# Taking the even part of a sum out of its PSUM bank with ScalarE, and adding the edge product with GpSimd

## The chip, the cores and the metric

The kernel runs on one core of one Trainium2 chip. The metric is the device time of one execution in microseconds (us). Every ratio below is to the kernel before, run on the same chip in the same rounds.

The engines are called by the names in the profile: PE is TensorE (PEld its weight loads), DVE is VectorE, ACT is ScalarE, POOL is GpSimd, SP is the engine whose queue issues transfers.

## The reference

An input of 8 x 3008 x 256 goes through a two-dimensional Fourier transform, of which the real part is kept, and then through a feed-forward layer with a squared relu:

```python
X = np.fft.fft(x, axis=1)
X = np.fft.fft(X, axis=2)
x = X.real.reshape(8 * 3008, 256)
h = np.maximum(x @ w_in, 0.0)         # w_in: 256 x 2048
out = (h * h) @ w_out                 # w_out: 2048 x 256
```

The real part of row k and that of the mirrored row S - k are, but for an edge term, an even part plus or minus an odd part. So the kernel works on half of the rows and makes the hidden values of a row and of its mirror from the same two products.

## The kernel before

The second transform is folded into the weights: `G1` holds the even (cosine) combination of `w_in`, `G2` the odd (sine) one, and `G3` is -2 times `G2` with its edge row set to zero. `PQ[b][0]` and `PQ[b][1]` are the even and odd parts of the transformed input. Row pairs are worked in chunks of 512 (`CH`; two chunks of 256 at the start, a short one of 264 at the end). A chunk has 16 units `u`, one per 128 hidden features. Its 128 or so matmuls of the second product (`po`) are interleaved with those of the first (`xb`) of the next chunk, so that PE never has to stop (it has no idle time from 100 to 600 us).

A unit in `x_front` costs PE three matmuls of 512 columns into one bank: even, odd, then, after ACT has read the bank with a relu, -2 times odd into the same bank, which ACT reads again for the mirror. A unit in `x_split` costs PE only two, into two banks, and pays for it on ACT and DVE:

```python
def x_front(c, u):                                   # cut
    for sn, G in ((0, G1), (1, G2)):
        mm(xb[...], G[:, fs], PQ[b][sn][...], ...)
    act(r_s(c, u), xb, AF.Relu)                      # L605
    return (c, u, xb, None)

def x_split(c, u):                                   # cut
    xs = [psx.tile([P, 512], F32, name=nm, tag="x")[:, 0:n] for nm in ("xo", "xe")]
    for t, G, sn in ((xs[0], G2, 1), (xs[1], G1, 0)):
        mm(t[...], G[:, fs], PQ[b][sn][...], ...)
    act(bs[0], xs[0], AF.Copy, bias=0.0, scale=1.0)  # L629

    def add():                                       # one step later
        stt(out=bs[1], in0=ebc[c][:, 0:n], scalar=gE2[:, u : u + 1], in1=bs[0], op0=ALU.mult,
            op1=ALU.subtract)                        # L632
        def sat(o, t):                               # L636: min(max(in0 + in1, 0), BIG)
            nc.vector._custom_dve(TENSOR_ADD_SAT, out=o, in0=xs[1], in1=t, s0=BIG, s1=0.0)
        sat(r_s(c, u)[:, 0, :], bs[0])
        relu_d(c, u, lambda o, i: sat(o[:, 0, :], bs[1]))

def x_back(cur):                                     # two steps later, cut
    if xb is None: return
    mm(xb[...], G3[:, fs], PQ[b][1][...], False, True)
    relu_d(c, u, lambda o, i: act(o, xb[:, :, i], AF.Relu))     # L651

def x_square(cur):                                   # per two units, cut
    if u // 2 in PLAN[c][1]: ...                     # a few on ACT, in two halves
    else: vt(h2, h2, h2, op=ALU.mult)                # L663, 128 x 2048, SBUF to SBUF

YZ = [(0, 0)] * 3 + [(2, 0)] * 3 + [(5, 1)] * 9 + [(7, 1)] * 9 + [(0, 0)]
```

`YZ` says how many of a chunk's 16 units are split, chunk by chunk: none, 2, 5, 7. `ebc[c]` is the edge row of the odd part, broadcast to all partitions by a transfer on POOL's queue, and `gE2` the edge weights.

## Time and profile before

| | before |
|---|---|
| time | 630.06 us (629.28 to 631.47, 4 runs) |
| PE busy, share of the span | 96% |
| DVE, ACT, POOL busy | 85%, 76%, 11% |
| units split (two matmuls instead of three) | 114 |

These lines are from the page of the kernel before: the busy times, the busy tenths of 40 slices for PE and DVE, the chain of waits, and the groups of instructions (line, engine, operation, out<-in, shapes, count | busy us, mean ns | idle time of the engine ahead of them).

```profile
PE 606.4 (96%) x4682; PEld 446.9 (71%) x4682; DVE 536.8 (85%) x827; ACT 479.3 (76%) x872; POOL 68.8 (11%) x97
...
PE   3969999999999999999999999999999999999997
...
DVE  8788799995988989889899879998999899999920
...
PE 92%; DVE 6%; ACT 1%; issue 0%; DVEq 0%; POOL 0%; POOLq 0%; ACTq 0%
...
L663 DVE TENSOR_TENSOR h<-h 128x2048 f16<-128x2048 f16 (+1 forms) x174 | 207.8, 1195 | 41.1 <-ACT h L651 36.5
...
L636 DVE CUSTOM_DVE_ANT_0 h<-xe,bs 128x512 f16<-128x512 f32 x228 | 145.9, 680 | 0.0
...
L632 DVE SCALAR_TENSOR_TENSOR bs<-eb,gE,bs 128x512 f32<-128x512 f16 x114 | 85.0, 745 | 9.1 <-ACT bs L629 8.4
L629 ACT ACTIVATE bs<-xo 128x512 f32<-128x512 f32 x114 | 68.5, 601 | 21.0 <-PE xo L73 16.3
```

PE is at nine tenths or more in all but three slices (the first, the third and the last), and the chain that ended last is 92% PE: the kernel is bound by TensorE. The mean of a saturating add is 680 ns, of the edge operation 745, of a square 1195 over all shapes (1219 for the full shape in the middle of the run). A split unit therefore costs DVE about 2.1 us and ACT a copy of 0.60 us, and saves PE one 512-column matmul.

The busy times in two stretches (PE, PEld, DVE, ACT and POOL busy us with the number of instructions, granted clock, share of the DMA engines, GB/s):

```profile
200.00:400.00 200.00, 200.00 (x1573) 148.00 (x1572) 174.34 (x258) 158.63 (x278) 14.67 (x19) 1.00 0.35 64
400.00:550.00 150.00, 150.00 (x1188) 115.53 (x1187) 140.96 (x191) 116.83 (x203) 4.83 (x9) 1.00 0.32 50
```

PE has no idle time at all there. By the groups of matmuls about 118,000 columns pass in 50 us, 2.36 per ns, so a 512-column matmul is worth 0.217 us. DVE is busy 87% and 94% of these stretches.

### The profile page before, as it was taken

What the parts mean: (1) busy time and instruction counts of PE and PEld (TensorE: products, weight loads), DVE (VectorE), ACT (ScalarE), POOL (GpSimd) and SP (SyncE); (2) the same over time, 40 slices, a digit from 0 to 9 for tenths busy, and PEclk for the clock granted to TensorE, in tenths of its full rate; (3) what the DMA queues carried; (4) which work ended last, traced back from release to release, by engine and by line L of the source; (5) the groups of instructions that cost most, each with busy time, mean ns of one, the idle gap of its engine ahead of it and who ended that gap; (6) DMA issues with size and microseconds to landing.
All of it is one profiled execution on the core that took longest, in us unless ns stands there. A gap on an engine that the chain in (4) does not pass through costs nothing.

```text
span 628.5 us, 11983 instructions
## 1 busy us (share of the span) xinstructions
PE 606.4 (96%) x4682; PEld 446.9 (71%) x4682; DVE 536.8 (85%) x827; ACT 479.3 (76%) x872; POOL 68.8 (11%) x97
## 2 busy tenths in 40 slices
PE   3969999999999999999999999999999999999997
PEld 1547677776777777777777768777787778877786
DVE  8788799995988989889899879998999899999920
ACT  6768887777788788777887877877877778878871
POOL 8204043120120005000000000000000000000000
PEclk9979999999999999999999999999999999999999
DMA  8944477682591416714313314314233134131112
GB/s 282 300 83 138 120 181 205 156 225 57 91 208 36 59 44 170 138 34 59 43 51 44 57 34 63 43 47 48 54 56 43 51 43 59 52 46 48 52 52 68
DMA packets 37342, 57.21 MB, mean 91 GB/s; under 512 B 7262, under 2 KB 31490, under 8 KB 37286
## 3 DMA queue, kind: packets, MB, share of 16 engines
q0 software_dynamic: 7536, 30.21, 27.9%
q1 hardware_dynamic: 29702, 26.23, 13.4%
q8 instruction: 36, 0.59, 0.4%
q14 instruction: 20, 0.16, 0.1%
q10 hardware_dynamic: 48, 0.02, 0.0%
HBM read 29.02 MB, written 24.64 MB: 85 GB/s over the span
## 4 chain that ended last, share of the span: by engine, by line
PE 92%; DVE 6%; ACT 1%; issue 0%; DVEq 0%; POOL 0%; POOLq 0%; ACTq 0%
PE po L73 52%; PE xb L73 25%; PE pf L73 6%; PE xo L73 4%; PE xe L73 4%; DVE h L663 2%; PE warm L73 1%; DVE u L330 1%; DVE v L342 0%; DVE w L348 0%; DVE wout L723 0%; DVE tm L248 0%; ACT h L605 0%; DVE tm L236 0%; DVE tt L183 0%
## 5 line engine op out<-in xcount | busy, mean ns | idle before, releaser
L73 PE MATMUL po<-wout,h 128*128 128x256 f16 x3024 | 433.6, 273 | 0.0
L73 PEld LDWEIGHTS <-h 128*128 128x128 f16 x3024 | 287.2, 98 | 113.9 <-issue 0.4
L663 DVE TENSOR_TENSOR h<-h 128x2048 f16<-128x2048 f16 (+1 forms) x174 | 207.8, 1195 | 41.1 <-ACT h L651 36.5
L605 ACT ACTIVATE h<-xb 128x512 f16<-128x512 f32 (+1 forms) x270 | 159.2, 590 | 67.8 <-PE xb L73 67.1
L73 PE MATMUL xb<-qt,G 128*128 128x512 f16 (+11 forms) x720 | 203.6, 322 | 4.9 <-ACT h L605 4.1
L651 ACT ACTIVATE h<-xb 128x512 f16<-128x512 f32 (+2 forms) x286 | 160.4, 567 | 20.3 <-PE xb L73 13.9
L73 PEld LDWEIGHTS <-G 128*128 128x128 f16 x1384 | 130.3, 98 | 36.7 <-issue 9.6
L636 DVE CUSTOM_DVE_ANT_0 h<-xe,bs 128x512 f16<-128x512 f32 x228 | 145.9, 680 | 0.0
L73 PE MATMUL xb<-pt,G 128*128 128x512 f16 (+9 forms) x360 | 103.8, 324 | 0.3 <-DVE qt L424 0.2
L632 DVE SCALAR_TENSOR_TENSOR bs<-eb,gE,bs 128x512 f32<-128x512 f16 x114 | 85.0, 745 | 9.1 <-ACT bs L629 8.4
L629 ACT ACTIVATE bs<-xo 128x512 f32<-128x512 f32 x114 | 68.5, 601 | 21.0 <-PE xo L73 16.3
L557 ACT ACTIVATE os<-po 128x512 f32<-128x512 f32 x94 | 56.4, 600 | 19.1 <-PE po L73 16.7
L614 POOL DMA_DIRECT2D eb<-qt x28 | 15.4, 551 | 349.6 <-DVE bs L632 297.1
L73 PE MATMUL xo<-qt,G 128*128 128x512 f16 (+14 forms) x152 | 43.4, 327 | 0.0
L73 PE MATMUL xe<-pt,G 128*128 128x512 f16 (+14 forms) x152 | 43.4, 326 | 0.0
L330 DVE TENSOR_TENSOR u<-x 127x765 f16<-127x765 f32 x32 | 29.7, 945 | 0.0
L101 POOL DMA_INDIRECT x<-in_x_dram,idx x18 | 27.6, 1536 | 5.8 <-issue 4.5
L73 PEld LDWEIGHTS <-w 127*128 127x128 f16 (+1 forms) x192 | 21.6, 118 | 7.2 <-issue 1.4
L73 PE MATMUL pf<-cosT,w 127*128 127x377 f16 (+1 forms) x96 | 20.5, 327 | 2.0 <-DVE cosT L279 2.0
L124 POOL DMA_DIRECT2D x<-in_x_dram x14 | 7.9, 562 | 123.3 <-DVE u L334 122.7
L348 DVE TENSOR_TENSOR w<-v 127x381 f16<-127x381 f16 x64 | 20.7, 352 | 0.0
L73 PE MATMUL pf<-sinT,w 127*127 127x377 f16 (+1 forms) x96 | 20.7, 323 | 0.0
(103 smaller groups left out, 216.9 us busy)
## 6 DMA issues: line engine op xcount, KB each, us to landing
out_dram<-os SPq DMA_DIRECT2D x157, 128.0 KB
x<-in_x_dram POOLq DMA_DIRECT2D x14, 756.0 KB, 9.6
wst<-in_moe_w_in_dram POOLq DMA_DIRECT2D x4, 512.0 KB, 6.9
wot<-in_moe_w_out_dram POOLq DMA_DIRECT2D x4, 512.0 KB, 9.1
eb<-qt POOLq DMA_DIRECT2D x14, 128.0 KB, 6.7
x<-in_x_dram SPq DMA_DIRECT2D x2, 756.0 KB
x<-in_x_dram,idx POOLq DMA_INDIRECT x18, 10.7
gE<-G SPq DMA_DIRECT2D x16, 0.2 KB
```

The lines of the kernel that those rows point to most:

```text
L73: nc.tensor.matmul(o, l, r, start=start, stop=stop, skip_group_check=True)
L101: nc.gpsimd.indirect_dma_start(out=x4[0:NP, 2 + s, q : q + rows, :].rearrange("p q d -> p (q d)"), out_offset=None, in_=bass.AP(tensor=x.t ...
L330: return lambda: vt(u[k, s, q0 : q0 + NQ // 2, 1:D], x4[k, s, q0 : q0 + NQ // 2, 1:D], x4[k, 3 - s, ::-1, :][:, q0 : q0 + NQ // 2, D - 1 : ...
L348: return lambda: vt(w[k, i, q : q + 3, 0 : P - 1], vs[s][k, q : q + 3, 1:P], vs[s][k, q : q + 3, D - 1 : P : -1], op=ALU.add if i < 2 else ...
L557: act(os_, po, AF.Copy, bias=0.0, scale=HS * HS)
L605: act(r_s(c, u), xb, AF.Relu)
L614: nc.gpsimd.dma_start(out=ebc[c][:, o : o + l], in_=PQ[b][1][P - 1 : P, i : i + l].unsqueeze(1).to_broadcast([1, P, l]))
L629: act(bs[0], xs[0], AF.Copy, bias=0.0, scale=1.0)
L632: stt(out=bs[1], in0=ebc[c][:, 0:n], scalar=gE2[:, u : u + 1], in1=bs[0], op0=ALU.mult, op1=ALU.subtract)
L636: nc.vector._custom_dve(TENSOR_ADD_SAT, out=o, in0=xs[1], in1=t, s0=BIG, s1=0.0)
L651: relu_d(c, u, lambda o, i: act(o, xb[:, :, i], AF.Relu))
L663: vt(h2, h2, h2, op=ALU.mult)
```

## The change

The intent is to let more units go with two matmuls by making them cheaper on DVE. `x_take` replaces `x_split`. PE writes only the even part E to a bank. ACT copies it out, times -2, into SBUF (T). DVE forms the edge product X in SBUF; POOL adds it, T = T + X. Two steps later PE adds the odd part to the bank in place, ACT reads the sum with a relu, and one saturating add on DVE of the bank and T makes the mirror. The signs of `G1` and `G2` are turned for that. A taken unit now costs DVE one product and one saturating add, and POOL one add. Where POOL is busy with input loads (`xbusy`), or the plan says so, DVE makes the sum out of the bank instead.

```diff
-    YZ = [(0, 0)] * 3 + [(2, 0)] * 3 + [(5, 1)] * 9 + [(7, 1)] * 9 + [(0, 0)]
+    YQZ = [(0, 0, 0)] * 3 + [(2, 0, 0)] * 3 + [(0, 9, 1)] * 9 + [(1, 10, 1)] * 9 + [(6, 0, 0)]
...
+    def x_take(c, u, si):
+        ...
+        for (b, i, o, l) in segs:
+            mm(xb[:, o : o + l], G1[:, fs], PQ[b][0][:, i : i + l], o == 0, True)
+        X = h2v(c, u)[:, u % 2, n : 2 * n]
+        ts(out=X, in0=ebc[c][:, 0:n], scalar1=gE2[:, u : u + 1], scalar2=None, op0=ALU.mult)
+        if u in PLAN[c][1] and si not in xbusy:
+            act(T, xb, AF.Copy, bias=0.0, scale=-2.0)
+            nc.gpsimd.tensor_tensor(T, T, X, op=ALU.add)
+        else:
+            stt(out=T, in0=xb, scalar=-2.0, in1=X, op0=ALU.mult, op1=ALU.add)
+        return (c, u, xb.unsqueeze(1), T)
...
     def x_back(cur):
+        if T is not None:
+            ...
+                mm(xb[:, 0, o : o + l], G2[:, fs], PQ[b][1][:, i : i + l], False, True)
+            act(r_s(c, u), xb, AF.Relu, scale=-1.0)
+            relu_d(c, u, lambda o, i: nc.vector._custom_dve(
+                TENSOR_ADD_SAT, out=o[:, 0, :], in0=xb[:, 0, i], in1=T[:, i], s0=BIG, s1=0.0))
             return
...
-            nc.gpsimd.dma_start(out=ebc[c][:, o : o + l],
+            nc.sync.dma_start(out=ebc[c][:, o : o + l],
...
+    def ewide(o):                      # 65 weight columns in place of 3
+        return eflat[k, o : o + MW]
```

Cut: the turned signs, the plan function (units that would need an edge row too early are left out), the earlier issue of most edge rows (six steps ahead in place of three), the place of three small tiles, and the wider weights of the last chunk's short group. 184 units are taken (178 of 512 columns, 6 of 264), 156 of them through ACT and POOL, 28 on DVE.

## The prediction

> **What bounds it now.** TensorE. The view of stretches shows PE 100% busy from 100 to 600 us; by groups, about 118,000 moving columns pass per 50 us, 2.36 columns per ns (512 columns start every 0.217 us in the timeline). The chain of waits is 92% PE. DVE is 87 to 95% busy there, ACT 77 to 80%, POOL 2 to 4%.

> **What changes.** In before, 114 "split" units spend two banks and two 512-column matmuls in place of three; each costs ACT one copy (601 ns) and DVE an edge operation (745) and two saturating adds (680 each), 2.03 us start to start. After, the instruction order shows 178 full and 6 264-column units taken. Each has two matmuls, one bank; ACT: relu (about 600) and, in 156, the copy (601); DVE: one tensor_scalar f16 128x512 (the same form, the G3 line, takes 352; estimate 0.2 to 0.3 us start to start), one saturating add; POOL: 156 tensor_tensor 128x512; 28 do the sum on DVE (about 0.75). Edge-row broadcasts move from POOL's queue to SP's.

> **Cost by engine.**
> - PE, critical: 64 x 512 + 6 x 264 columns go = 14.6 us at 2.36/ns. Widening the 3-column weights removes a gap of about 0.2 us at each of 8 groups (timeline at 374 us), about 1.5 us. Floor about 630.3 - 16 = 614.
> - DVE: -231 us, +121 +64 +20: about 510 busy, from 537.
> - ACT: 92 more 512-wide passes, +55 us busy: about 530; back to back they start every 0.48 us, so about 19 us per 22 us chunk.
> - POOL: the only measured tensor_tensor is 128x128, 873 ns, but DVE held it: it ended 0.31 us after a DVE tensor_tensor ended, so I estimate 1.1 to 1.2 us for 512[...]. 156 x 1.15 = 180 us, half of the time from chunk 6 on.

> **The risk.** [...] POOL's operations stretch until DVE's end, and a DVE pass of 460 ns took 630 when POOL ran. Per late chunk the excluding work would be 10 x 1.15 (POOL) + 7 x 1.15 (squares) + 11 x 0.25 = 22.3 us, against 22.2 us of PE. If the exclusion is strict, each POOL add holds a square up by some 0.5 us, DVE needs about 24 us per late chunk, and the gain is gone. If it is milder, or the adds fall under the saturating adds (one SBUF input), PE stays the bound. The plan (10 of 16 on POOL, none near the x loads) looks balanced for that: I expect 4 us lost of 16.

> **Prediction: 618.5 us, 612 to 633 eight times in ten.** Faster by over 2% (below 617.7) 0.48; within 2% 0.42; slower 0.10.

> **What would show it.** Right: PE near 100% busy in 100 to 600 us at 2.36 columns/ns, DVE near 83% plus stretched squares, ACT near 86%, POOL 30 to 40%; chain over 90% PE. Exclusion: mean of the squares (1219 ns now) or of the new tensor_scalar (0.35) well above these, POOL adds over 1.3 us.

> **What would make it wrong.** Squares stretched by 0.4 us or more: DVE becomes the bound, PE waits for banks, and the time is 625 to 640. ACT late with the mid-sum copy, so that the odd matmul waits. Edge rows late where batches meet. If POOL adds cost nobody anything: 613 to 615.

630.3 us, less 16 for PE, plus 4 for the exclusion, is 618.3, put as 618.5. What stands of the exclusion is what the trace of the kernel before shows between 6 and 9 us; that it holds for squares and products was the assumption, and so was how strict it is. The 1.1 to 1.2 us for an add of 512 columns is the estimate; four times the 0.31 us that the 128-column add took after DVE's end would be 1.24.

## The result, and the profile after

| | before | after |
|---|---|---|
| time | 630.06 us (629.28 to 631.47) | 638.44 us (638.14 to 638.82) |
| ratio to before | | 1.0125 (1.0109 to 1.0141) |
| matmuls in the trace | 4682 | 4596 |
| PE, DVE, ACT, POOL busy us | 606, 537, 479, 69 | 595, 570, 517, 248 |

Times are medians of 4 runs each. A ratio is the mean time of one kernel's fast runs over that of the other's of the same rounds, with a 95% interval, so it is not quite the ratio of the medians.

The matmuls went as planned, and the kernel is 1.25% slower. The same lines of the page after:

```profile
PE 595.0 (93%) x4596; PEld 440.6 (69%) x4596; DVE 569.7 (89%) x887; ACT 516.8 (81%) x952; POOL 248.1 (39%) x226
...
PE   3869999999999998999999999999999999998997
...
DVE  7788798986799999999999986999999999998861
...
PE 50%; DVE 31%; issue 7%; ACT 6%; DMA 4%; POOL 1%; SPq 0%; DVEq 0%; ACTq 0%; POOLq 0%
...
L648 POOL TENSOR_TENSOR bs<-bs,h 128x512 f32<-128x512 f32 x156 | 196.5, 1260 | 261.0 <-DVE h L645 163.7
L680 DVE TENSOR_TENSOR h<-h 128x2048 f16<-128x2048 f16 (+1 forms) x174 | 250.1, 1439 | 13.5 <-ACT h L668 13.3
...
L661 DVE CUSTOM_DVE_ANT_0 h<-xb,bs 128x512 f16<-128x512 f32 (+2 forms) x190 | 123.9, 655 | 21.5 <-ACT h L660 21.4
...
L647 ACT ACTIVATE bs<-xb 128x512 f32<-128x512 f32 x156 | 95.2, 610 | 14.1 <-PE xb L73 11.7
L645 DVE TENSOR_SCALAR h<-eb,gE 128x512 f16<-128x512 f16 (+1 forms) x184 | 78.2, 429 | 1.3 <-DMA eb<-qt 1.1
```

PE's row has eights in three places that were nines, DVE is at nine tenths or more in most slices of the middle, and the chain is now 50% PE and 31% DVE. DVE's busy time rose by 33 us, though its planned work fell. The rise is in two groups: the squares (L680 here, L663 before) went from 1195 to 1439 ns in the mean, with the same shapes and count, and the new product (L645) takes 429 ns. POOL's add takes 1260 ns in the mean.

```profile
200.00:400.00 200.00, 190.86 (x1500) 141.94 (x1498) 188.22 (x273) 171.07 (x309) 89.21 (x73) 1.00 0.33 63
400.00:550.00 150.00, 144.38 (x1148) 111.13 (x1147) 147.55 (x202) 131.56 (x236) 76.09 (x62) 1.00 0.29 51
```

In these stretches PE is idle 9.1 and 5.6 us, and DVE, without the gaps of before, is busy 94% and 98% of the time. What PE waits for is a square (from the view of waits: who waited for whom, us in total, times, the longest):

```profile
PEld L73 <- DVE h L680: 19.1, 14, 2.5
...
PE po L73 <- DVE h L680: 15.3, 13, 2.2
```

That a square takes longer says nothing yet of the cause. The timeline of 7 us in a late chunk (start us, length us, engine, line, operation, shapes) shows how it is lengthened; rows of other engines and the other rows of DVE are left out:

```profile
506.90 1.15 POOL L648 TENSOR_TENSOR bs<-bs,h 128x512 f32<-128x512 f32 x1 [3.29 <-ACT h L668]
...
506.99 2.14 DVE L680 TENSOR_TENSOR h<-h 128x2048 f16<-128x2048 f16 x1
...
509.54 1.16 POOL L648 TENSOR_TENSOR bs<-bs,h 128x512 f32<-128x512 f32 x1 [1.49 <-ACT bs L647]
...
509.92 1.86 DVE L680 TENSOR_TENSOR h<-h 128x2048 f16<-128x2048 f16 x1
```

The add on POOL runs from 506.90 to 508.05. A square starts at 506.99 and ends at 509.13, which is 1.08 us after the add's end. The next add runs from 509.54 to 510.70, a square starts at 509.92 and ends at 511.78, again 1.08 us after. A full square alone takes 1.22 us, so both ended as if they had begun only when the add was nearly over: they look not slowed but held.

The stretch adds up. Squares: 97 x 0.443 = 43 us; products: 184 x (429 - 344) ns = 16 us, where 344 is their mean in the first experiment below; two groups of folding operations on the inputs, 64 x (482 - 352) and 32 x (1058 - 945) ns, 12 us. That is 71 us of DVE time; by DVE's busy time (569.7 us here, 501.3 without the add, in the first experiment) it is 68.

One small part of the change did what it was to do. The matmuls with 3 columns of weights used to be followed and led by a pause. In the timeline of PE before,

```profile
142.95 0.60 PE L73 MATMUL po<-wout,h 128*128 128x256 f16 x4
143.48 0.64 PE L73 MATMUL pf<-cosT,eall 127*3 127x377 f16 x3
144.06 0.39 PE L73 MATMUL xb<-pt,G 128*128 128x512 f16 x1
```

and after, with 65 columns of weights:

```profile
142.87 0.60 PE L73 MATMUL po<-wout,h 128*128 128x256 f16 x4
143.31 0.65 PE L73 MATMUL pf<-cosT,eall 127*65 127x377 f16 x3
143.79 0.38 PE L73 MATMUL xb<-pt,G 128*128 128x512 f16 x1
```

From the start of the four second-product matmuls to the start of the matmul behind the group of three it was 1.11 us and is 0.92. Eight groups make 1.5 us.

### The profile page after: what moved, and what is told of

The parts are those of the page before. It is cut to its first block, busy times and chain, and to the rows that moved or that the text cites. A ratio compares the mean times of both kernels' runs of the same rounds, so it can differ in the third digit from the quotient of the medians.

```text
span 636.7 us, 12358 instructions
## 1 busy us (share of the span) xinstructions
PE 595.0 (93%) x4596; PEld 440.6 (69%) x4596; DVE 569.7 (89%) x887; ACT 516.8 (81%) x952; POOL 248.1 (39%) x226
## 4 chain that ended last, share of the span: by engine, by line
PE 50%; DVE 31%; issue 7%; ACT 6%; DMA 4%; POOL 1%; SPq 0%; DVEq 0%; ACTq 0%; POOLq 0%
PE po L73 29%; PE xb L73 17%; DVE h L680 12%; DVE h L661 7%; DVE h L645 4%; PE pf L73 3%; DMA eb<-qt 2%; DVE u L335 2%; DVE w L353 1%; DMA wst<-in_moe_w_in_dram 1%; DVE v L347 1%; ACT h L660 1%; ACT bs L647 1%; ACT h L618 1%; ACT h L668 1%
## 5 line engine op out<-in xcount | busy, mean ns | idle before, releaser
L73 PE MATMUL po<-wout,h 128*128 128x256 f16 x3024 | 455.6, 274 | 15.3 <-DVE h L680 15.3
L648 POOL TENSOR_TENSOR bs<-bs,h 128x512 f32<-128x512 f32 x156 | 196.5, 1260 | 261.0 <-DVE h L645 163.7
L680 DVE TENSOR_TENSOR h<-h 128x2048 f16<-128x2048 f16 (+1 forms) x174 | 250.1, 1439 | 13.5 <-ACT h L668 13.3
L73 PE MATMUL xb<-qt,G 128*128 128x512 f16 (+16 forms) x786 | 221.2, 322 | 7.7 <-ACT h L618 4.1
L618 ACT ACTIVATE h<-xb 128x512 f16<-128x512 f32 (+1 forms) x200 | 119.1, 595 | 49.9 <-PE xb L73 49.6
L73 PE MATMUL xb<-pt,G 128*128 128x512 f16 (+16 forms) x512 | 147.0, 324 | 1.4 <-DVE h L661 0.8
L661 DVE CUSTOM_DVE_ANT_0 h<-xb,bs 128x512 f16<-128x512 f32 (+2 forms) x190 | 123.9, 655 | 21.5 <-ACT h L660 21.4
L668 ACT ACTIVATE h<-xb 128x512 f16<-128x512 f32 (+1 forms) x210 | 119.9, 576 | 13.5 <-PE xb L73 7.6
L660 ACT ACTIVATE h<-xb 128x512 f16<-128x512 f32 (+1 forms) x184 | 111.1, 604 | 11.1 <-PE xb L73 6.1
L647 ACT ACTIVATE bs<-xb 128x512 f32<-128x512 f32 x156 | 95.2, 610 | 14.1 <-PE xb L73 11.7
L645 DVE TENSOR_SCALAR h<-eb,gE 128x512 f16<-128x512 f16 (+1 forms) x184 | 78.2, 429 | 1.3 <-DMA eb<-qt 1.1
L335 DVE TENSOR_TENSOR u<-x 127x765 f16<-127x765 f32 x32 | 33.2, 1058 | 1.3 <-DMA x<-in_x_dram,idx 1.3
L73 PE MATMUL pf<-cosT,w 127*128 127x377 f16 (+1 forms) x96 | 21.1, 334 | 1.0 <-DVE cosT L281 1.0
L677 ACT ACTIVATE h<-h 128x1024 f16<-128x1024 f16 x18 | 18.9, 1052 | 3.0 <-DVE h L661 3.0
```

The source lines that it names most:

```text
L73: nc.tensor.matmul(o, l, r, start=start, stop=stop, skip_group_check=True)
L335: return lambda: vt(u[k, s, q0 : q0 + NQ // 2, 1:D], x4[k, s, q0 : q0 + NQ // 2, 1:D], x4[k, 3 - s, ::-1, :][:, q0 : q0 + NQ // 2, D - 1 : ...
L618: act(r_s(c, u), xb, AF.Relu, scale=-1.0)
L645: ts(out=X, in0=ebc[c][:, 0:n], scalar1=gE2[:, u : u + 1], scalar2=None, op0=ALU.mult)
L647: act(T, xb, AF.Copy, bias=0.0, scale=-2.0)
L648: nc.gpsimd.tensor_tensor(T, T, X, op=ALU.add)
```

## The experiments

Times are medians of 4 runs each; the kernel before, run in the same rounds, was at 629.43 to 630.45 us in the median.

Theory A, exclusion: a POOL add that reads SBUF and a DVE operation with two SBUF inputs (squares, folds), or the one-input product (754 ns where an add runs in the change, 339 where none does), shut each other out for a whole instruction. Rivals: (1) DVE or ACT simply has too much to do, or the order of DVE's instructions ties it to ACT; (2) the chain of copy, add and saturating add is too long, so banks come free late; (3) any work on POOL holds DVE up, reading or not.

For the progress of a kernel I use the start of the second-product matmuls, of which every full chunk has 128: "per late chunk" is the time from the 1920th to the 2688th, over six. It is 23.60 us before and 24.07 after.

### 1. The add left out

```diff
             act(T, xb, AF.Copy, bias=0.0, scale=-2.0)
-            nc.gpsimd.tensor_tensor(T, T, X, op=ALU.add)
```

> The changed kernel without the GpSimd add (wrong on purpose: the edge product is missing in 156 units); ScalarE's copy, VectorE's product and everything else stay. Exclusion theory (a GpSimd add and VectorE's squares and products shut each other out of SBUF): the mean of the squares falls from 1439 to about 1200 ns, the product from 429 to about 350, and the time to 613 to 618 us. Rival 1 (VectorE or ScalarE is simply given too much, or the order of VectorE's stream couples it to ScalarE): the time stays at 632 to 639. Rival 2 (the chain copy, add, saturating add is too long): also falls here; the next run tells it from exclusion.

Measured: 617.35 us (616.18 to 617.54), ratio to before 0.9801 (0.9784 to 0.9819). The result is wrong, on purpose (relative error 0.065). A late chunk takes 22.84 us. The page:

```profile
PE 79%; DVE 9%; DMA 6%; ACT 3%; issue 2%; POOL 1%; SPq 0%; DVEq 0%; ACTq 0%; POOLq 0%
...
L679 DVE TENSOR_TENSOR h<-h 128x2048 f16<-128x2048 f16 (+1 forms) x174 | 207.4, 1193 | 14.2 <-ACT h L667 14.0
...
L645 DVE TENSOR_SCALAR h<-eb,gE 128x512 f16<-128x512 f16 (+1 forms) x184 | 62.5, 344 | 3.2 <-DMA eb<-qt 3.1
```

The squares are back at 1193 ns, the product at 344, and 21.1 us of 638.44 are gone (20.4 by the two ratios to before), with ACT's copies, DVE's products and the order of everything else in place. Rival 1 falls. Rival 2 does not yet, for the chain is shorter too; but in the trace of the change the view of waits shows no DVE, ACT or PE instruction of the chunks that waits for a POOL add, which speaks against it.

### 2. The same chain, but POOL only writes

```diff
-            nc.gpsimd.tensor_tensor(T, T, X, op=ALU.add)
+            for _ in range(2):
+                nc.gpsimd.iota(T, pattern=[[0, n]], base=0, channel_multiplier=0, ...)
```

> The changed kernel with the GpSimd add replaced by two fills of the same tile that read nothing (wrong on purpose), about 0.6 us each, so the chain and GpSimd's busy time stay about the same. Exclusion theory: squares near 1200 ns, time 613 to 620 us; the product[...] may still be stretched. Rival 2 (length of the chain): 635 to 640 us, saturating adds wait for the fills.

Measured: 618.60 us (617.16 to 620.36), ratio 0.9826 (0.9803 to 0.9849); wrong (0.585). A late chunk takes 22.84 us.

```profile
PE 84%; DVE 7%; ACT 3%; DMA 3%; POOL 1%; issue 1%; SPq 0%; DVEq 0%; ACTq 0%; POOLq 0%
...
L649 POOL IOTA bs<- 128x512 f32 x312 | 175.3, 568 | 262.7 <-ACT bs L647 250.6
...
L682 DVE TENSOR_TENSOR h<-h 128x2048 f16<-128x2048 f16 (+1 forms) x174 | 207.1, 1192 | 13.9 <-ACT h L670 13.7
...
L645 DVE TENSOR_SCALAR h<-eb,gE 128x512 f16<-128x512 f16 (+1 forms) x184 | 78.1, 429 | 3.9 <-DMA eb<-qt 3.8
```

Two fills of 568 ns take about as long as the add did, and T passes through POOL as before. The fills do not read X, so they wait for ACT's copy alone; yet DVE's saturating adds did wait for them, 13.9 us in all, so the chain was not made easier. The squares stay at 1192 ns: 92 of them overlap a fill and take 1215 ns, 74 do not and take 1216. The product is stretched to the same mean as by the add (429 ns), in another way: 101 full products meet a fill and take 503 ns, where 40 met an add and took 754. Run 2 is 1.25 us slower than run 1, with intervals that overlap: about that much of the 21.1 us, at most, is POOL's presence and the chain. The other 19.8 us (18.8 by the ratios) went when the add no longer read SBUF. Rivals 2 and 3 fall, the latter except for the product.

### 3 and 4. POOL work that nobody waits for, in the kernel before

Run 3 adds to each of the 114 split units of the kernel before one POOL add that reads ACT's copy and writes a tile nobody reads; run 4 adds two fills in its place, paced by a copy of one column.

```diff
         act(bs[0], xs[0], AF.Copy, bias=0.0, scale=1.0)
+        nc.gpsimd.tensor_tensor(dum[0][:, 0:n], bs[0], bs[0], op=ALU.add)     # run 3
+        nc.gpsimd.tensor_copy(dum[0][:, 0:1], bs[0][:, 0:1])                  # run 4
+        for _ in range(2):
+            nc.gpsimd.iota(dum[0][:, 0:n], pattern=[[0, n]], ...)
```

> The kernel before plus one GpSimd add per split unit (114, 128x512, reads the copied bank, writes a dummy that nobody reads). Nothing waits for it but the reuse of the copy's buffer. Exclusion theory: squares and edge operations of VectorE are stretched by 0.3 to 0.5 us where an add runs, VectorE goes from 90% to about 98% busy and the time rises to 640 to 655 us. If exclusion costs little: 629 to 633 us.

> The control of the run before: the same GpSimd busy time, but as two fills of the dummy that read nothing (one 128x1 copy paces them). Exclusion theory: squares stay near 1200 ns and the time at 629 to 634 us. If any GpSimd work, reading or not, holds VectorE up: as with the reading adds, 640 to 655 us.

Measured: 648.16 us (646.99 to 649.28), ratio 1.0294 (1.0272 to 1.0317), with the adds; 642.75 (642.63 to 644.81), ratio 1.0216 (1.0195 to 1.0237), with the fills. The squares went as theory A says: 1291 ns in the mean with the adds (60 that overlap one 1502, the others 1215), 1196 with the fills. The time did not, for the control lost 13 us with squares as short as before. As a test of the time the pair is inconclusive. The control's progress shows where its time went: it runs 1.4 us ahead of before at the 384th second-product matmul, 4.6 behind at the 512th, level from there to the 1024th and 10.1 behind at the 1152nd, and nearly level again. Run 3 has its two jumps at the same places. DVE waits there for the edge row (view of waits, run 4):

```profile
DVE bs L639 <- DMA eb<-qt: 15.4, 7, 8.3
```

In the kernel before, the edge rows are broadcast by transfers on POOL's queue, where the added work stands ahead of them. That this queue is the cause of the jumps is argued from these waits; run 12 was made to be free of it.

### 5. A repair without POOL

ACT takes the even part out as in the change; product and sum are one DVE pass from SBUF to SBUF, two steps later, just ahead of the saturating add. 8 and 10 units per chunk.

```diff
-    ... [(0, 9, 1)] * 9 + [(1, 10, 1)] * 9 ...
+    ... [(0, 8, 1)] * 9 + [(0, 10, 1)] * 9 ...
...
             act(T, xb, AF.Copy, bias=0.0, scale=-2.0)
-            nc.gpsimd.tensor_tensor(T, T, X, op=ALU.add)
+            return (c, u, xb.unsqueeze(1), T, True)
...
     def x_back(cur):
+            if len(cur) > 4:
+                stt(out=T, in0=ebc[c][:, 0:n], scalar=gE2[:, u : u + 1], in1=T, op0=ALU.mult, op1=ALU.add)
             act(r_s(c, u), xb, AF.Relu, scale=-1.0)
```

> A repair without GpSimd: ScalarE takes the even part out as in the change, but the edge product and the sum are one VectorE pass from SBUF to SBUF (as in the kernel before, 0.66 us start to start), done two steps later, just ahead of the saturating add; 8 of 16 units in the early chunks and 10 in the late ones. Exclusion theory: squares 1200 to 1220 ns, nothing on GpSimd to wait for; VectorE about 22.3 us per late chunk against 22.4 of TensorE, so 618 to 625 us. If the loss had come from ScalarE's mid-sum copy or from the one bank held through the chain: no better than 632 us.

Measured: 629.10 us (627.90 to 629.95), ratio 0.9973 (0.9956 to 0.9989), correct. The squares are at 1194 ns, as expected, but the time is above the range I gave. The chain is 61% PE and 31% DVE and a late chunk takes 23.71 us. DVE's busy time in it is 22.31 us, just what I had counted. What I had not counted is a gap of 136 ns between each product-and-sum and the saturating add that reads its result: 60 of them in six late chunks, 1.36 us per chunk. Busy time and gaps make 23.67 of the 23.71 us, so with 10 units DVE's own sequence is the bound.

### 6. Fewer POOL adds, some sums on DVE, more squares on ACT

```diff
-    ... [(0, 9, 1)] * 9 + [(1, 10, 1)] * 9 ...
+    ... [(3, 5, 2)] * 9 + [(4, 6, 2)] * 9 ...
```

> The changed kernel with fewer GpSimd adds: 5 (early) and 6 (late) of 16 units on GpSimd, 3 and 4 summed by VectorE out of the bank, one more pair of squares per chunk on ScalarE. Exclusion theory: the adds then fit under the passes of VectorE that do not shut GpSimd out; squares near 1350 ns, time 616 to 624 us. If the exclusion were not what costs: the time follows the number of taken units and VectorE's own work alone, 617 to 620.

Measured: 632.63 us (630.80 to 632.89), ratio 1.0025 (1.0009 to 1.0042), correct. A miss: the squares did come down, to 1249 ns, and the number of taken units is that of run 5, yet the time is worse. The chain now holds 15% ACT, and DVE's saturating adds wait 45 us for ACT's relu. Three things were changed at once here, so the run doesn't say which of them moved the bound to ACT, and it tells nothing for or against A.

### 7. The add in two halves

```diff
-            nc.gpsimd.tensor_tensor(T, T, X, op=ALU.add)
+            for r in (slice(0, n // 2), slice(n // 2, n)):
+                nc.gpsimd.tensor_tensor(T[:, r], T[:, r], X[:, r], op=ALU.add)
```

> The changed kernel with each GpSimd add cut into two of 256 columns. Exclusion theory: a square that meets an add waits for the rest of a half only, so squares fall from 1439 to 1300 to 1380 ns and the time to 626 to 635 us, though GpSimd's own work grows. If the length of one add does not matter: 638 us or more.

Measured: 630.17 us (629.31 to 631.76), ratio 1.0000 (0.9982 to 1.0019), correct.

```profile
L649 POOL TENSOR_TENSOR bs<-bs,h 128x256 f32<-128x256 f32 x312 | 295.6, 971 | 155.8 <-DVE h L645 74.0
...
L681 DVE TENSOR_TENSOR h<-h 128x2048 f16<-128x2048 f16 (+1 forms) x174 | 227.5, 1309 | 13.8 <-ACT h L669 13.6
```

The result and the taken units are those of the change, POOL is busy 99 us longer, and the kernel is 8.3 us faster. More squares meet POOL (107), but each loses less: 1406 ns where one meets a half, against 1659. 102 of these squares start while a half add runs, and 93 of them end within 10 ns of 1081 ns after that half's end, so what a square loses is the rest of the instruction that POOL has begun. The products gain nothing by it (504 ns in the mean, 429 in the change).

### 8. The same units, all summed by DVE

```diff
-    ... [(0, 9, 1)] * 9 + [(1, 10, 1)] * 9 ...
+    ... [(9, 0, 1)] * 9 + [(11, 0, 1)] * 9 ...
```

> The changed kernel with the same units taken, but all summed by VectorE out of the bank (product, sum and saturating add: 1.6 us per unit), none by ScalarE and GpSimd. VectorE needs about 25.6 us per late chunk against 22.2 of TensorE, so it is the bound by its own work: 648 to 668 us. Exclusion theory: squares back at 1200 to 1220 ns all the same. If it is below 638, GpSimd is a worse place for the sum than VectorE itself even at this many units.

Measured: 673.27 us (672.02 to 674.32), ratio 1.0673 (1.0655 to 1.0691), correct. Squares 1192 ns, DVE 55% of the chain, a late chunk 26.92 us. So for this plan POOL is a better place for the sum than DVE: exclusion makes the adds dear, not worthless.

### 9, 10 and 11. Fewer units, so that TensorE is the bound again

Run 9 and run 10 keep the half adds and take 8 and 10, or 7 and 8, units per chunk; run 11 is the repair without POOL with 7 and 9. None takes units in the short last chunk.

```diff
+    ... [(0, 8, 1)] * 9 + [(0, 10, 1)] * 9 + [(0, 0, 0)]      # run 9
+    ... [(0, 7, 1)] * 9 + [(0, 8, 1)] * 9 + [(0, 0, 0)]       # run 10
+    ... [(0, 7, 1)] * 9 + [(0, 9, 1)] * 9 + [(0, 0, 0)]       # run 11
```

> Half adds as in the run before, but 8 (early) and 10 (late) of 16 units taken, none of them summed by VectorE by plan, and no unit taken in the short last chunk. By the half adds' stretch (about 0.3 us of VectorE per taken unit) VectorE needs about 21.3 us per late chunk and TensorE 22.4: TensorE is the bound again and the time 620 to 626 us. If VectorE stays above 97% busy there: 627 to 631.

> The same with 7 and 8 units. Fewer matmuls saved (2 us less early, 4 us less late), less exclusion. If the run with 8 and 10 is bound by TensorE, this one is slower than it by 3 to 5 us; if that one is still bound by VectorE, this one is the faster of the two, 622 to 626.

> The repair without GpSimd with 7 (early) and 9 (late) units and none in the last chunk: VectorE has 1.35 us less to do per chunk than in its first version, TensorE 0.22 more. 622 to 627 us.

| run | time | ratio to before | late chunk |
|---|---|---|---|
| 9, half adds, 8 and 10 | 623.74 us (623.21 to 626.10) | 0.9898 (0.9854 to 0.9942) | 23.18 us |
| 10, half adds, 7 and 8 | 625.36 us (624.66 to 625.54) | 0.9912 (0.9874 to 0.9950) | 23.39 us |
| 11, no POOL, 7 and 9 | 625.40 us (625.18 to 626.34) | 0.9921 (0.9882 to 0.9959) | 23.36 us |

All three are correct and beat the kernel before by about 1% and the change, by the ratios, by about 2%. The intervals overlap, so they are not told apart: after the repair the plan that leaves POOL out (run 11) does as well as those that use it. The page of run 9:

```profile
PE 84%; DVE 8%; ACT 3%; issue 1%; DMA 1%; POOL 1%; DVEq 0%; ACTq 0%; POOLq 0%
...
L649 POOL TENSOR_TENSOR bs<-bs,h 128x256 f32<-128x256 f32 x298 | 262.5, 903 | 182.8 <-DVE h L645 85.0
L681 DVE TENSOR_TENSOR h<-h 128x2048 f16<-128x2048 f16 (+1 forms) x174 | 226.0, 1300 | 25.2 <-ACT h L669 22.1
```

The chain is 84% PE again (92% before), though the squares are still stretched to 1300 ns. Run 10 was expected 3 to 5 us behind run 9 and is 1.6 behind, so run 9 doesn't have all that its saved matmuls are worth.

### 12. The cleaner form of run 3

Two dummy adds per split unit in the kernel before, in the last nine full chunks only, where no input load shares POOL's queue; the edge rows on SP's queue.

```diff
-            nc.gpsimd.dma_start(out=ebc[c][:, o : o + l],
+            nc.sync.dma_start(out=ebc[c][:, o : o + l],
...
+        for _ in range(2 if c >= 15 else 0):
+            nc.gpsimd.tensor_tensor(dum[0][:, 0:n], bs[0], bs[0], op=ALU.add)
```

> A cleaner version of the third run: the kernel before with two dummy GpSimd adds (each reads the copied bank twice and writes a tile that nobody reads) per split unit of the last nine full chunks only, where no x load shares GpSimd's queue, and with the edge-row broadcasts on SP's queue. Nothing waits for a dummy but the reuse of the copy's buffer. Exclusion theory: up to 380 us the trace runs as before; after that most squares are stretched to 1500 to 1800 ns, VectorE goes from 94% to 98% or more busy, and the time is 640 to 665 us. If GpSimd's adds only matter through the results that VectorE waits for: 628 to 633 us, squares at 1219.

Measured: 661.34 us (660.71 to 662.49), ratio 1.0492 (1.0464 to 1.0521), correct. Up to the 1664th second-product matmul it runs 1.1 us ahead of before, with no jump; from there it falls back to 30.6 us behind, at 27.07 us per late chunk. The groups of DVE between 420 and 620 us:

```profile
L668 DVE TENSOR_TENSOR h<-h 128x2048 f16<-128x2048 f16 x51 | 79.6, 1561 | 2.0
L641 DVE CUSTOM_DVE_ANT_0 h<-xe,bs 128x512 f16<-128x512 f32 x104 | 66.3, 676 | 0.0
L637 DVE SCALAR_TENSOR_TENSOR bs<-eb,gE,bs 128x512 f32<-128x512 f16 x52 | 56.5, 1087 | 0.0
```

No result of these adds is used, and the view of waits has none of ACT or PE for POOL in the whole run, and one of DVE, at the start. The squares stand at 1561 ns (1219 before) and the edge operation, which also has two SBUF inputs, at 1087 (746 before), while the saturating add, with one, takes 676 (681 before). DVE is busy 99% of this stretch. Exclusion alone slows the kernel before, without any longer chain and without another load on DVE or ACT. The edge rows were moved in the whole run, without loss in the part that has no adds.

## Why the prediction was wrong

- **What bounds before: right.** PE had no idle time between 100 and 600 us and was 92% of the chain.
- **What the change takes off PE: right.** By the view of stretches and the groups, the rate stays at 2.33 to 2.35 columns per ns where PE is not idle (2.36 before). Without the add a late chunk takes 22.84 us, 0.76 less than before; four fewer 512-column matmuls at 0.217 us are 0.87. The 1.5 us for the wider weights showed too: 0.19 us for each of eight groups. The floor of 614 us was not reached even without the add (617.35). Of the 3.4 us between, some are lost where the plan steps up and at the short last chunk, where the progress of run 1 stops gaining on before; what is lost there was not tested.
- **What ACT can bear: right.** ACT's busy time rose by 38 us (55 were predicted), a copy takes 610 ns (601 before), and it delayed nobody enough to matter, as run 1, which keeps it, shows.
- **POOL's add: right in size.** The estimate was 1.1 to 1.2 us; where no DVE operation held it up it took 1.15 to 1.16.
- **The exclusion: this step failed.** The text had evidence of the exclusion in the trace of before. These are lines that it used, from the start of the kernel before:

```profile
7.83 0.75 DVE L248 TENSOR_TENSOR tm<-tm,tt 128x567 f32<-128x567 f32 x1
8.02 0.87 POOL L198 TENSOR_TENSOR md<-md,td 128x128 f32<-128x128 f32 x1
...
8.61 0.63 DVE L183 TENSOR_SCALAR tt<-tm 128x567 int32<-128x567 int32 x1
```

POOL's add starts at 8.02, while a DVE addition of two SBUF tiles runs until 8.58, and ends 0.31 us after that; the DVE pass that starts at 8.61 takes 0.63 us, where f32 passes of that size had taken 0.46.

The text even costed the strict case: "DVE needs about 24 us per late chunk, and the gain is gone". It measured 24.07. But then it took the milder case, "I expect 4 us lost of 16", and its reason for that was no measurement: "The plan (10 of 16 on POOL, none near the x loads) looks balanced for that". The look of the plan outweighed the numbers. In its place the runs showed 21.1 us lost to the add, 19.8 of them because it reads SBUF (runs 1 and 2, against the change's 638.44), and the strict case: a square that starts during an add ends 1081 ns after it, 76 times of 80 within 10 ns.
- **The size of the strict case: the time was in its range, the sum behind it was not complete.** It gave 625 to 640 us for squares stretched by 0.4 us or more; the time was 638 with a mean stretch of all squares of only 0.24. The squares that meet an add lose 0.44 us, but the products (16 us) and the folds (12 us) are stretched too, and the text gave that no cost.
- **The hope that adds fall under the saturating adds: wrong in this order of instructions.** 97 of 166 squares met an add. An add starts when a product has been made and a copy has landed, soon after which DVE's next square comes up; nothing in the program keeps the two apart, and an add of 1.16 us doesn't fit under a saturating add of 0.68.

## What to carry to other kernels

When work moves from VectorE to GpSimd, cost it on both engines: here one add of 1.16 us on GpSimd took 0.44 us of VectorE (68 us, the difference in VectorE's busy time between run 1 and the change, over 156 adds), where the same sum on VectorE itself takes 0.69 (run 8, 512 columns). Add the times of all operations that exclude each other, here GpSimd's adds, VectorE's passes with two SBUF inputs (squares that met an add took 1659 ns, the others 1216), and the one-input product (754 and 339 ns), and compare the sum with the time of a stage; if it is near, expect the waits to be real and cut the GpSimd work short (halves won back 8 us) or take fewer units (1% better than before). And when the trace and the arithmetic agree on a loss, don't discount it because the program looks tuned.
